# Spectral filter and mixer in one kernel: the first batch's row order, and where the length-64 sets and the u tile's parts stand

## The chip, the cores and the metric

The kernel runs on one core of a Trainium2 chip. The core's engines are TensorE (PE, matmuls; PEld is its weight load), VectorE (DVE), ScalarE (ACT), GpSimd (POOL) and SyncE (SP), which only issues DMAs here. Each engine works through its own instructions in the order in which the program gives them. The metric is the device time of one execution in microseconds (us).

## The reference, cut to what matters

x has 8 batches of 3008 rows (the sequence) by 256 columns. A real Fourier transform along the sequence is multiplied by a filter and transformed back; then comes one mixer layer over tokens and one over channels.

```python
X = np.fft.rfft(x, axis=1)                 # 8 x 1505 x 256
y = np.fft.irfft(X * (filt_r + 1j * filt_i)[None], n=3008, axis=1)
xt = y.transpose(0, 2, 1)
h = np.maximum(xt @ w_tok1, 0.0) @ w_tok2  # 3008 -> 256 -> 3008
u = y + h.transpose(0, 2, 1)
out = u + np.maximum(u @ w_ch1, 0.0) @ w_ch2   # 256 -> 1536 -> 256
```

x, the filter and the weights come in as float64 and are turned into float32 on the chip.

## The kernel before, in words

**Transform.** 3008 is 64 x 47. The transform is made in two stages, one of length 64 (tables `wa`, `was`) and one of length 47 folded to 24 (`wbi`), and goes back the same way; the last step, of length 64 again, is not made on its own but added into the u tile (`wai`). Batch 0 (`first`) runs alone at the start, while ScalarE, VectorE and TensorE also convert the weights to float32 (`convert_middle`, `convert_end`). Batch 1 uses whole 128-row matmuls (`a_unit`). Batches 2 to 7 are `tiled`: their length-64 stage consists of six *sets* (`a_pair`, called by `sets` in `dft`), each of eight matmuls on 64 x 64 quarters of the array, of which four run side by side. Ahead of each set VectorE makes a sum and a difference of the rows (`x_sums`, line 559, tile `sd`, two instructions; the sds lie alternately in two buffers). A set fills two PSUM banks, either those called acc and b (`turn`) or the two `pg` banks; ScalarE copies them out (line 550) and SP stores them to `z_tmp` (line 552).

**Rows of g.** What comes back from the length-47 stage is stored to `g_tmp` and read again as `t4` tiles of 128 rows. In before, all batches store these rows in two halves (`h k g`), the first batch too, which writes each piece with two DMAs from ScalarE's queue (line 697) and reads each part with two DMAs (`t4_load`, line 793).

**Mixer.** For each batch there are six tiles of output columns (m = 0 to 5, 512 wide, the last 448) and for each six steps over the hidden channels (jp = 0 to 5); an *item* is one (b, m, jp). In `mix`, an item issues on TensorE: `up_first` (line 1019, with u and v tiles into the pg banks), the first `down` part of the item before (line 1053, po banks, from hh), `up_last` (line 1035), and the second and third part of `down` (from t). VectorE (helper `v`, line 997) makes u2 (out: hh) and s from the pg banks, t from hh, and after `up_last` two additions "hh<-ps_pg,s", which free the pg banks; ScalarE applies the relu (line 1040).

**The u tile of the next m** is made meanwhile in parts by `u_quarter`: part 0 and 1 are pairs of matmuls (line 924), part 2 is `u_sets`, 32 small products on 64 x 64 quarters (line 904), and three pairs more; part 3 is empty. Then come `u_turn` (two VectorE steps on u) and `v_steps` (three on v), which wait in the list `todo_v` until `one_step` issues them. The v tile is what `up_first` of the next m needs after its first pair of matmuls. The tables `own` (same batch) and `new` (first m of the next batch) say at which place of which jp each part is issued. `finish` puts the steps that end an output tile into the same list.

**Token product.** Once a batch, at item n-4, `token_product` (line 850) goes through twelve blocks of token weights, which `w1_load` (line 827) brings from `w1_tmp` into a ring of seven.

**What sets the order.** The whole is under a manual schedule: every engine and every DMA queue keeps the order in which the Python code issues. `mix` yields at places 0, 1, 1.5, 1.7 and 2 of each item, and at each of these the table at the end (lines 1379 to 1381) decides whether the transform of a later batch, a generator, takes a step: "s" is one `x_sums`, "e" one set, "d" two sets, "c" the copies of the pair's acc and b banks. Before the change a tiled batch takes, in the last m of one batch, s at jp 3, 4, 5 and e at jp 4 and 5; in the first m of the next, s at jp 0, d at jp 1, c, s at jp 2 and 3, d at jp 4, c. `w_load` brings a filter tile, after `zero_rows` has cleared it on GpSimd (line 596).

**First batch's end.** `token_sums` (line 799) is its token product; `w2_load` (line 366) brings parts of w_tok2 through GpSimd's queue; `turn_out` (line 965) makes sums of w_tok2 on GpSimd.

Of the kernel before, what the change touches and what calls it, by code (L numbers as in the profile page):

```python
# [17 lines left out]
B = 8  # L18
# [41 lines left out]
def _make_tables():  # L60
# [12 lines left out]
    by_half = wai.reshape(K2, 2, 2, P).transpose(1, 0, 2, 3).reshape(P, P)  # L73
    wa, wait = wa.reshape(P, P), by_half.T
    wai = np.concatenate((by_half[:, one], by_half[:, two][:, ::-1]), axis=1)
# [46 lines left out]
    for e in range(2):  # L122
        for h in range(2):
# [4 lines left out]
            wbi.astype(f), wbi0.astype(f))  # L128
# [3 lines left out]
def kernel(  # L132
# [13 lines left out]
    wa_np, was_np, wa0_np, wai_np, wait_np, wbi_np, wbi0_np = _make_tables()  # L146
# [4 lines left out]
    wait_d = nc.inline_tensor(np.ascontiguousarray(wait_np), name="wait_t").ap()  # L151
    wbi_d = nc.inline_tensor(wbi_np, name="wbi_t").ap()
# [5 lines left out]
    z_d, g_d = ([nc.dram_tensor("%s_tmp%d" % (what, g), shape + (len(bs), D), FP32, kind="Internal").ap()  # L158
                 for g, bs in enumerate(GROUPS)] for what, shape in (("z", (P, A)), ("g", (2, K2, KH))))
# [367 lines left out]
    def rows_of(t_d, b):  # L527
        g, i = place_of[b]
        return t_d[g].rearrange("h k (g a) b d -> (h k g) a b d", a=A)[:, :, i, :]
# [42 lines left out]
    def dft(bs):  # L572
# [48 lines left out]
        def sets(i, n):  # L621
            return [a_pair(*u, sd, tags) for u, sd, tags in zip(todo[i:i + n], sums[i:], (turn, ("pg", "pg")))]

        if tiled:
            next_sum()
            yield "s"
            next_sum()
            for i in range(2):
                yield "e"
                sets(i, 1)[0]()  # L630
                yield "s"
                next_sum()
            for i in (2, 4):
                yield "d"
                leave, leave_pg = sets(i, 2)
                leave_pg()
                if i == 2:
                    zero_rows(0)
                    w_load(0)
                yield "c"  # L640
                leave()
                for _ in range(2 * (i == 2)):
                    yield "s"
                    next_sum()
            yield "w"
# [36 lines left out]
        def bi_unit(k):  # L682


            ps = bank(free_bank()).rearrange("p (b d) -> p b d", b=2)[:, 0:nb, :]
            for i, p in enumerate(prods.pop(k)):
                wi = turn_i[:, k // WC % 4, k % WC] if i else wbs[k // WC][:, TI:TI + 2 * KR:2, k % WC]
                nc.tensor.matmul(ps[0:KR], wi, p, start=(i == 0), stop=(i == 1))
            c, r = divmod(k, KC)
            if r == 0:  # L690
                where, tag = (p2p, "p2") if c % 3 == 2 else (t3p, "t3")
                t3s[c] = where.tile([KR, KC, nb, D], FP32, tag=tag, name="t3")
            by_block(t3s[c][:, r], ps[0:KR])
            if r == KC - 1:
                t3 = t3s.pop(c)
                for h in range(2):
                    nc.scalar.dma_start(g_d[0][h, ts(c, KC)].rearrange("k r b d -> r k b d"), t3[ts(h, KH)])
# [91 lines left out]
    def t4_load(b, c, lo=PARTS[0], hi=P, queue=nc.sync):  # L789
        if lo == 0:  # L790
            t4[b, c] = t4p.tile([P, TC4, D], FP32, tag="t4", name="t4")
        for to in [slice(lo, hi)] if hi - lo == P else [slice(h * HALF + lo // 2, h * HALF + hi // 2) for h in range(2)]:
            queue.dma_start(t4[b, c][to], rows_of(g_d, b)[to, ts(c, TC4), :])
# [32 lines left out]
    def w1_load(j):  # L826
        nc.sync.dma_start(w1_ring[:, j % W1S], w1_d[j])
# [129 lines left out]
    def w2_sums(m):  # L957
# [211 lines left out]
    def mix(next_ready):  # L1169
# [11 lines left out]
        own = ({(3, 0): (0,), (3, 2): (1,)}, {(2, 2): (0,), (3, 0): (1,), (3, 2): (2, 3)})  # L1181
        new = {(JP - 2, 0): (0, 1), (JP - 1, 0): (2, 3)}
# [20 lines left out]
        for i in range(len(items) + 1):  # L1203
# [84 lines left out]
    with tc.manual_schedule():  # L1288
# [71 lines left out]
        for b, i, place in mix(next_ready):  # L1360
# [57 lines left out]
```

## Time and profile before

| | us |
|---|---|
| three timed runs | 2429.73, 2432.22, 2433.08 (median 2432.22) |
| profiled execution | 2427.55 |
| its span, first to last instruction | 2425.7 |
| granted TensorE clock, mean | 0.993 |
| first mixer matmul at | 153 |
| one batch to the next (wait for v at 1032.2 and 1317.7) | 285.5 |

In the lines of the profile, L12 is line 12 of the kernel. A group reads: engine, line, operation, out<-in by tile names, partitions x elements, count. A timeline row begins with the start and the duration of the row in us; "x2" is two instructions merged into one row, and in brackets stands how long the engine had been idle before and what ended that. Float32 matmuls are recorded as two passes each. Matmuls overlap, so the step from one start to the next says what one costs: 0.216 us for a pass of 256 columns. Idle time of an engine that is not the bottleneck costs nothing.

### The profile page before, as it was taken

How to read it: one execution, taken by the hardware profiler on the slowest of the kernel's cores; microseconds unless marked ns; L12 is line 12 of the kernel's file. 1: busy time of each engine (PE TensorE's matmuls, PEld its weight loads, DVE VectorE, ACT ScalarE, POOL GpSimd, SP SyncE). 2: the span in 40 equal slices, each digit the busy share in tenths (PEclk: the TensorE clock that was granted, in tenths of full speed). 3: DMA queues.
4: the chain of work that ended last, by engine and by line, in shares of the span. 5: the costliest groups of instructions: out<-in, count | busy, mean ns of one | idle time of the engine just before them, and what ended most of it. 6: DMA issues, size and time to landing. Idle time of an engine off the chain costs nothing.

```text
span 2425.7 us, 41188 instructions
## 1 busy us (share of the span) xinstructions
PE 2366.4 (98%) x15148; PEld 1979.3 (82%) x15148; DVE 2006.1 (83%) x3753; ACT 689.4 (28%) x1339; POOL 708.8 (29%) x1138
## 2 busy tenths in 40 slices
PE   7899999999999999999999999999999999999998
PEld 4567788888897888978888888888889788898887
DVE  6788888788887888788887788878888798877887
ACT  5723222222223222232222222222222222212222
POOL 7465754131222122212212311321132113122122
PEclk8999999999999999999999999999999999999999
DMA  9774355533363334633435443634345433331101
GB/s 214 212 203 129 94 182 197 152 112 98 106 193 117 107 101 117 187 122 98 111 113 182 119 113 92 192 117 124 89 110 185 127 107 105 109 131 32 47 15 21
DMA packets 190143, 302.31 MB, mean 125 GB/s; under 512 B 43156, under 2 KB 126458, under 8 KB 184566
## 3 DMA queue, kind: packets, MB, share of 16 engines
q1 hardware_dynamic: 142942, 237.58, 31.9%
q0 software_dynamic: 40128, 55.28, 9.6%
q10 hardware_dynamic: 6872, 6.82, 0.9%
q8 instruction: 120, 1.97, 0.4%
q14 instruction: 81, 0.66, 0.1%
HBM read 215.37 MB, written 83.62 MB: 123 GB/s over the span
## 4 chain that ended last, share of the span: by engine, by line
PE 84%; DVE 3%; issue 0%; ACT 0%; DVEq 0%; ACTq 0%
PE ps_po L1053 33%; PE ps_pg L1019 19%; PE ps_pg L1035 14%; PE ps_acc L924 3%; PE ps_b L850 3%; PE ps_b L534 3%; PE ps_acc L850 2%; PE ps_pg L534 2%; PE ps_b L924 2%; PE ps_acc L904 2%; DVE u L997 1%; DVE hh L997 1%; DVE t L997 1%; DVE v L997 0%; PE ps_b L904 0%
## 5 line engine op out<-in xcount | busy, mean ns | idle before, releaser
L1065 POOL DMA_DIRECT2D out_dram<-r x738 | 453.2, 624 | 1386.1 <-issue 991.5
L1040 ACT ACTIVATE hh<-hh 128x512 f32<-128x512 f32 (+1 forms) x576 | 347.9, 621 | 1036.0 <-DVE hh L997 1032.1
L997 DVE TENSOR_TENSOR hh<-ps_pg,s 128x512 f32<-128x512 f32 (+3 forms) x864 | 481.9, 585 | 113.7 <-ACT s L1022 101.8
L1053 PE MATMUL ps_po<-t,wc 128*128 128x256 f32 (+1 forms) x2296 | 558.8, 380 | 0.9 <-DVE t L997 0.8
L1053 PEld LDWEIGHTS ps_po<-t,wc 128*128 128x128 f32 x2296 | 424.8, 190 | 99.2 <-issue 41.0
L1019 PE MATMUL ps_pg<-v,wc 128*128 128x256 f32 (+1 forms) x1728 | 419.0, 379 | 11.6 <-DVE v L997 11.6
L1053 PE MATMUL ps_po<-hh,wc 128*128 128x256 f32 (+1 forms) x1722 | 412.7, 376 | 0.6 <-POOL wc L393 0.6
L1019 PEld LDWEIGHTS ps_pg<-v,wc 128*128 128x128 f32 x1728 | 325.7, 191 | 61.6 <-DVE v L997 25.4
L1053 PEld LDWEIGHTS ps_po<-hh,wc 128*128 128x128 f32 x1722 | 328.0, 191 | 38.9 <-POOL wc L393 1.4
L1035 PE MATMUL ps_pg<-u,wc 128*128 128x256 f32 (+1 forms) x1152 | 292.3, 376 | 3.1 <-DVE hh L997 2.6
L997 DVE TENSOR_TENSOR t<-t,hh 128x256 f32<-128x256 f32 (+1 forms) x576 | 251.5, 437 | 19.8
L1035 PEld LDWEIGHTS ps_pg<-u,wc 128*128 128x128 f32 x1152 | 216.6, 190 | 36.5 <-DVE hh L997 10.3
L997 DVE TENSOR_TENSOR s<-ps_pg,hh 128x512 f32<-128x512 f32 (+1 forms) x288 | 196.1, 681 | 31.1 <-PE ps_pg L1019 0.8
L1022 ACT COPY s<-ps_pg 128x256 f32<-128x256 f32 (+1 forms) x288 | 106.0, 368 | 329.2 <-PE ps_pg L1019 327.7
L997 DVE TENSOR_TENSOR t<-hh 128x512 f32<-128x512 f32 (+1 forms) x288 | 195.1, 677 | 0.6 <-ACT hh L1040 0.6
L1019 PE MATMUL ps_pg<-u,wc 128*128 128x256 f32 (+1 forms) x576 | 169.7, 376 | 4.4 <-DVE hh L997 4.0
L1035 PE MATMUL ps_pg<-v,wc 128*128 128x256 f32 (+1 forms) x576 | 168.8, 375 | 0.0
L997 DVE TENSOR_TENSOR u<-ps_acc,u 128x256 f32<-128x256 f32 x84 | 46.8, 557 | 109.3 <-PE ps_acc L924 85.9
L1019 PEld LDWEIGHTS ps_pg<-u,wc 128*128 128x128 f32 x576 | 107.8, 190 | 22.0 <-DVE hh L997 8.5
L1035 PEld LDWEIGHTS ps_pg<-v,wc 128*128 128x128 f32 x576 | 108.7, 190 | 13.3 <-DVE s L997 0.4
L924 PE MATMUL ps_acc<-w 128*128 128x256 f32 x336 | 97.5, 392 | 0.0
L717 DVE TENSOR_TENSOR p<-ps_b,filt 128x1024 f32<-128x1024 f32 x56 | 68.4, 1222 | 14.2 <-PE ps_pg L534 13.3
(169 smaller groups left out, 2801.4 us busy)
## 6 DMA issues: line engine op xcount, KB each, us to landing
w<-w_tmp SPq DMA_DIRECT2D x42, 1024.0 KB
w<-w_tmp SPq DMA_DIRECT2D x84, 448.0 KB
out_dram<-r POOLq DMA_DIRECT2D x738, 32.0 KB, 4.0
g_tmp<-t SPq DMA_DIRECT2D x112, 192.0 KB
t<-g_tmp SPq DMA_DIRECT2D x42, 512.0 KB
t<-z_tmp SPq DMA_DIRECT2D x196, 96.0 KB
z_tmp<-t SPq DMA_DIRECT2D x72, 256.0 KB
wb<-wbi_t SPq DMA_DIRECT2D x56, 256.0 KB
```

Of the source, the lines that this page charges most:

```text
L534: nc.tensor.matmul(outs(i, j), stat(i, j), mov(i, j), start=True, stop=True)
L717: nc.vector.tensor_tensor(out=prods[c, h], in0=pss[h].unsqueeze(1).to_broadcast([P, 2, 2, D]), in1=filts[c % FB], op=ALU.mult)
L850: nc.tensor.matmul(ps[:, at], w[:, n], mov, start=(j == 0 and i in (0, 2)), stop=(j == AP - 1 and i >= 5))
L904: nc.tensor.matmul(pss[e][half_of(i), dh, ts(q, HALF)], t4[b, c][half_of(e), r, ds(dh * P + i * HALF, HALF)], wai[half_of(e), 0:HALF], sta ...
L924: nc.tensor.matmul(to, h1[:, n, :], w2_at(m, at), start=(i < 2 and j == 0), stop=(j >= 1))
L997: nc.vector.tensor_tensor(out=out, in0=in0, in1=in1, op=op)
L1019: nc.tensor.matmul(ps[:, 0:hw], chan[0][:, jp, n, :], mov, start=True, stop=True)
L1022: nc.scalar.copy(out=s[:, 0], in_=g[0][:, 0, 0:hw])
L1035: nc.tensor.matmul(ps[:, 0:hw], chan[0][:, jp, n, :], mov, start=True, stop=True)
L1040: nc.scalar.activation(out=hs, in_=hs, func=AF.Relu)
L1053: nc.tensor.matmul(po[i][:, j, 0:hw], chan[1][:, jp, n, :], mov, start=(jp == 0 and first == 1), stop=(jp == JP - 1 and last == 1))
L1065: q.dma_start(bass.AP(tensor=ob.tensor, offset=ob.offset + to, ap=ap + [[1, cw]]), of)
```

## The change

It has these parts:

1. The first batch keeps the order `(k, g)` of its rows; the table `wai` (and its transpose, with which w_tok1's conversion multiplies) follows. Writing and reading `g_tmp` takes one DMA instead of two. At item 28 the first 64 columns of `wai` are overwritten with the table for the later batches (`was_i`).
2. Later batches still use two halves, so `w1_load` reads the token weights with rows permuted, in two DMAs of 64 partitions.
3. `turn_out` does in three instructions what took six.
4. Parts 2 and 3 of the u tile (the 32 small products) are issued at place 1.5, between the second and the third part of `down`: for the same batch at jp 3 instead of jp 3 place 2, for the next batch at jp 4 instead of jp 5 place 0. Two `one_step` calls follow at jp 4 of the last m.
5. The six sets are taken as one, two, one, two instead of one, one, two, two. The two single ones stand at the places of part 4, right ahead of the small products, in the pg banks instead of acc and b. The sums are taken at jp 3 of the last m and at jp 0, 1, 2, 3, 4 of the first m. The clearing and loading of the first filter tile follows the fourth sum.

```diff
         if tiled:
             next_sum()
-            yield "s"
-            next_sum()
-            for i in range(2):
+            for i in (0, 3):
                 yield "e"
-                sets(i, 1)[0]()
-                yield "s"
-                next_sum()
-            for i in (2, 4):
+                sets(i, 1, (("pg", "pg"),))[0]()
+                for _ in range(2 if i == 0 else 1):
+                    yield "s"
+                    next_sum()
                 yield "d"
-                leave, leave_pg = sets(i, 2)
+                leave, leave_pg = sets(i + 1, 2, (turn, ("pg", "pg")))
                 leave_pg()
-                if i == 2:
-                    zero_rows(0)
-                    w_load(0)
                 yield "c"
                 leave()
-                for _ in range(2 * (i == 2)):
+                for _ in range(2 * (i == 0)):
                     yield "s"
                     next_sum()
+                    if len(sums) == 4:
+                        zero_rows(0)
+                        w_load(0)
...
-                t3 = t3s.pop(c)
-                for h in range(2):
-                    nc.scalar.dma_start(g_d[0][h, ts(c, KC)].rearrange("k r b d -> r k b d"), t3[ts(h, KH)])
+                nc.scalar.dma_start(g_d[0][ts(c, KC)].rearrange("k r b d -> r k b d"), t3s.pop(c))
...
-        for to in [slice(lo, hi)] if hi - lo == P else [slice(h * HALF + lo // 2, h * HALF + hi // 2) for h in range(2)]:
-            queue.dma_start(t4[b, c][to], rows_of(g_d, b)[to, ts(c, TC4), :])
+        queue.dma_start(t4[b, c][lo:hi], rows_of(g_d, b)[lo:hi, ts(c, TC4), :])
...
     def w1_load(j):
-        nc.sync.dma_start(w1_ring[:, j % W1S], w1_d[j])
+        rows = w1_d[j].rearrange("(k h g) s n -> h k g (s n)", h=2, g=2)
+        for h in range(2):
+            nc.sync.dma_start(w1_ring[half_of(h), j % W1S], rows[h])
...
         def turn_out():
-            for t in range(2):
-                pool(halves_of[:, t, 1], halves_of[:, t, 0], halves_of[:, t, 1])
-                pool(halves_of[:, t, 0], halves_of[:, t, 0], halves_of[:, t, 0], ALU.add)
-                pool(halves_of[:, t, 0], halves_of[:, t, 0], halves_of[:, t, 1])
+            pool(two, one, two)
+            pool(one, one, one, ALU.add)
+            pool(one, one, two)
...
-        own = ({(3, 0): (0,), (3, 2): (1,)}, {(2, 2): (0,), (3, 0): (1,), (3, 2): (2, 3)})
-        new = {(JP - 2, 0): (0, 1), (JP - 1, 0): (2, 3)}
+        own = ({(3, 0): (0,), (3, 2): (1,)}, {(2, 2): (0,), (3, 0): (1,), (3, 1.5): (2, 3)})
+        new = {(JP - 2, 0): (0, 1), (JP - 2, 1.5): (2, 3)}
...
             yield b, i % n, 1.5
+            if now:
+                u_parts(b, m, jp, 1.5)
             if old:
                 down(mo, jo, 2, hhs.pop(i - 1), tts.pop(i - 1), pos[bo, mo])
...
                 u_parts(b, m, jp, 2)
+                if m + 1 == MT and jp == JP - 2 and b + 1 < B:
+                    one_step()
+                    one_step()
...
+                if i == 28:
+                    nc.sync.dma_start(wai[:, 0:HALF], was_i_d)
...
-                    "s": ((3, 1), (4, 1), (5, 1)) if tail else ((0, 1), (2, 1), (3, 1)),
-                    "e": ((4, 1.5), (5, 1.5)), "d": ((1, 1.5), (4, 1.5)), "c": ((2, 0), (5, 0)),
+                    "s": ((3, 1),) if tail else ((0, 1), (1, 1), (2, 1), (3, 1), (4, 1)),
+                    "e": ((4, 1.5),) if tail else ((3, 1.5),), "d": ((1, 1.5), (4, 1.5)), "c": ((2, 0), (5, 0)),
```

More of the change, by code (lines that the diff above doesn't have):

```diff
@@ L72, in _make_tables @@
         wai[k2] = wa[:, k2].T * (2.0 if k2 else 1.0)
-    by_half = wai.reshape(K2, 2, 2, P).transpose(1, 0, 2, 3).reshape(P, P)
-    wa, wait = wa.reshape(P, P), by_half.T
-    wai = np.concatenate((by_half[:, one], by_half[:, two][:, ::-1]), axis=1)
+    wait = wai.reshape(P, P).T
+    was_i = wai.reshape(K2, 2, 2, P).transpose(1, 0, 2, 3).reshape(P, P)[:, one]
+    wa, wai = wa.reshape(P, P), wai.reshape(P, P)
+    wai = np.concatenate((wai[:, one], wai[:, two][:, ::-1]), axis=1)
     n1 = A - 1 - np.arange(A)
@@ L127, in _make_tables @@
     return (wa.astype(f), np.concatenate((wa[one], wa[one])).astype(f), wa0.astype(f), wai.astype(f), wait.astype(f),
-            wbi.astype(f), wbi0.astype(f))
+            was_i.astype(f), wbi.astype(f), wbi0.astype(f))
 @with_exitstack
@@ L144 @@
     nc = tc.nc
-    wa_np, was_np, wa0_np, wai_np, wait_np, wbi_np, wbi0_np = _make_tables()
+    wa_np, was_np, wa0_np, wai_np, wait_np, was_i_np, wbi_np, wbi0_np = _make_tables()
     wa_d = nc.inline_tensor(wa_np, name="wa_t").ap()
@@ L151 @@
     wait_d = nc.inline_tensor(np.ascontiguousarray(wait_np), name="wait_t").ap()
+    was_i_d = nc.inline_tensor(np.ascontiguousarray(was_i_np), name="was_i_t").ap()
     wbi_d = nc.inline_tensor(wbi_np, name="wbi_t").ap()
@@ L157 @@
     place_of = {b: (g, i) for g, bs in enumerate(GROUPS) for i, b in enumerate(bs)}
-    z_d, g_d = ([nc.dram_tensor("%s_tmp%d" % (what, g), shape + (len(bs), D), FP32, kind="Internal").ap()
-                 for g, bs in enumerate(GROUPS)] for what, shape in (("z", (P, A)), ("g", (2, K2, KH))))
+    z_d, g_d = ([nc.dram_tensor("%s_tmp%d" % (what, g), shape[g > 0] + (len(bs), D), FP32, kind="Internal").ap()
+                 for g, bs in enumerate(GROUPS)]
+                for what, shape in (("z", ((P, A), (P, A))), ("g", ((K2, KR), (2, K2, KH)))))
     w2_d = nc.dram_tensor("w2_tmp", (MT, P, 4, 512), FP32, kind="Internal").ap()
@@ L528, in rows_of @@
         g, i = place_of[b]
-        return t_d[g].rearrange("h k (g a) b d -> (h k g) a b d", a=A)[:, :, i, :]
+        rows = "h k (g a) b d -> (h k g) a b d" if g else "k (g a) b d -> (k g) a b d"
+        return t_d[g].rearrange(rows, a=A)[:, :, i, :]
     def four(outs, stat, mov):
@@ L619, in next_sum, with sets @@
             more(1)
-        def sets(i, n):
-            return [a_pair(*u, sd, tags) for u, sd, tags in zip(todo[i:i + n], sums[i:], (turn, ("pg", "pg")))]
+        def sets(i, n, banks_of):
+            return [a_pair(*u, sd, tags) for u, sd, tags in zip(todo[i:i + n], sums[i:], banks_of)]
         if tiled:
             next_sum()
-            yield "s"
-            next_sum()
-            for i in range(2):
+            for i in (0, 3):
                 yield "e"
-                sets(i, 1)[0]()
-                yield "s"
-                next_sum()
-            for i in (2, 4):
+                sets(i, 1, (("pg", "pg"),))[0]()
+                for _ in range(2 if i == 0 else 1):
+                    yield "s"
+                    next_sum()
                 yield "d"
-                leave, leave_pg = sets(i, 2)
+                leave, leave_pg = sets(i + 1, 2, (turn, ("pg", "pg")))
                 leave_pg()
-                if i == 2:
-                    zero_rows(0)
-                    w_load(0)
                 yield "c"
                 leave()
-                for _ in range(2 * (i == 2)):
+                for _ in range(2 * (i == 0)):
                     yield "s"
                     next_sum()
+                    if len(sums) == 4:
+                        zero_rows(0)
+                        w_load(0)
             yield "w"
```

## The prediction

> **What bounds the kernel now.** I read the page first: busy shares, then the chain of work that ended last.
>
> ```profile
> PE 2366.4 (98%) x15148; PEld 1979.3 (82%) x15148; DVE 2006.1 (83%) x3753; ACT 689.4 (28%) x1339; POOL 708.8 (29%) x1138
> PE 84%; DVE 3%; issue 0%; ACT 0%; DVEq 0%; ACTq 0%
> ```
>
> TensorE is the bound, so a gain must come from its idle gaps, its array switches, or the first 150 us, which have other limits. The order of the built program shows the same 7576 matmuls and 3755 VectorE instructions after the change: work is moved, not removed. So I looked for what TensorE waits on (its own waits, longest of each kind last):
>
> ```profile
> PE ps_pg L1019 <- DVE v L997: 11.6, 7, 1.7
> ```
>
> Seven waits for v: one at each change of batch. The timeline there, TensorE then VectorE, for batch 2 to 3:
>
> ```profile
> 1032.20 0.59 PE L1019 MATMUL ps_pg<-u,wc 128*128 128x256 f32 x2
> 1034.53 1.56 PE L1019 MATMUL ps_pg<-v,wc 128*128 128x256 f32 x6 [1.74 <-DVE v L997]
> ...
> 1029.74 1.15 DVE L997 TENSOR_TENSOR hh<-ps_pg,s 128x448 f32<-128x448 f32 x2
> 1032.12 1.28 DVE L559 TENSOR_TENSOR sd<-filt 128x512 f32<-128x512 f32 x2
> 1033.33 0.68 DVE L997 TENSOR_TENSOR v<-u 128x512 f32<-128x512 f32 x1
> ```
>
> Without the wait the v matmuls would follow the u pair after 0.43 us; they come 2.33 after it: 1.90 lost. Between hh and v stand two u steps and a pair of sums (sd). Six of the seven look like this; the last (batch 6 to 7, no sets beside it) is different:
>
> ```profile
> 2172.95 0.67 PE L1019 MATMUL ps_pg<-u,wc 128*128 128x256 f32 x2 [0.48 <-DVE u L997]
> 2174.76 2.47 PE L1019 MATMUL ps_pg<-v,wc 128*128 128x256 f32 x6 [1.15 <-DVE v L997]
> ...
> 2175.28:2178.69 3.41, 3.41 (x10) 0.50 0.01 2
> ```
>
> After two gaps the granted clock is 0.50 for 3.41 us (last line, a stretch of the windows view: busy, clock, DMA share, GB/s). By start-to-start times TensorE loses there 0.65 and 1.39 waiting, then 0.97 and 0.82 at half clock: 3.8.
>
> **The change, part by part.** All steps below are start-to-start times of that timeline.
>
> *1. Batch change, six times.* u's parts 2 and 3 and the two u_turn steps come an item earlier, and two sums leave this stretch. From 1020.37, where the first down matmuls of item jp=4 start (0.85 with the switch to 64-row tiles, to 1021.22): the set now uses the pg banks, which the hh pair (1020.57 + 1.15 = 1021.72) must leave first, so its second half starts at 1021.78. Set 0.86 + 0.05, u's 32 small products 1.09, its three full pairs 1.40, down 0.76: 1025.94. Item jp=5 has 5.29 (1.51 + 1.135 + 1.135 + 1.51), then the u pair 0.43: TensorE is ready for v at 1031.66. VectorE: u adds and u_turn from 1025.36 for 1.21 + 1.32, to 1027.89; that is 0.58 later than hh could start (1.37 after 1025.94), so hh, s and the t sums end at 1030.31 (+2.42), hh pair 1.06, first v 0.72, second 0.44 + 0.06: v is there at 1032.59. TensorE still waits 0.93, but goes on at 1032.59 instead of 1034.53: -1.94. One set less is done by then; it returns in step 3.
>
> *2. First pair of sets in the new batch (jp=1).* Before, sums and sets are an item apart. Now the second set's sum is issued at (1, 1) and the pair at (1, 1.5), and VectorE's built order puts it behind hh and three finish steps:
>
> ```profile
> 1045.25 1.28 DVE L997 TENSOR_TENSOR hh<-ps_pg,s 128x512 f32<-128x512 f32 x2
> 1046.45 1.22 DVE L997 TENSOR_TENSOR u<-u,r 128x224 f32<-128x224 f32 x3
> ...
> 1046.50 1.16 PE L534 MATMUL ps_pg<-sd,was 64*64 64x512 f32 x8
> ```
>
> Both engines keep their distance from the v matmuls, so before's clock serves. The sum can start at 1046.45 + 1.13 = 1047.58 and ends, at 1.28 for two, at 1048.86. TensorE wants the second set at 1046.50 and all but its first quarter waits until 1048.92, then 0.86 + 0.16: down goes on at 1049.94 instead of 1047.59: +2.35. Queued behind on TensorE are the down matmuls and the whole next item.
>
> *3. The single set beside u's small products (3, 1.5).* New on this path: 0.86 + 0.05. It shares the switches of the small products (about 0.09 in and 0.22 out when a set stands alone). Its pg banks are free when the hh pair ends:
>
> ```profile
> 1060.70 1.28 DVE L997 TENSOR_TENSOR hh<-ps_pg,s 128x512 f32<-128x512 f32 x2
> ```
>
> 1062.04 against TensorE's 1061.61: 0.43. Together +1.34.
>
> *4. Second pair (jp=4).* The same as step 2; here hh and the two u_turn steps stand ahead of the sum:
>
> ```profile
> 1071.05 0.69 DVE L950 SCALAR_TENSOR_TENSOR u<-u 128x512 f32<-128x512 f32 x1
> ...
> 1071.14 1.04 PE L534 MATMUL ps_pg<-sd,was 64*64 64x512 f32 x8
> ```
>
> The sum runs 1071.65 to 1072.93, the set from 1072.99, down at 1074.01 instead of 1072.11: +1.90.
>
> Per batch -1.94 + 2.35 + 1.34 + 1.90 = +3.65; six batches: +21.9. Bounds: if VectorE were in time at both pairs, steps 2 and 4 are 0 (-3.6 in all); if each pair of sums takes the 1.54 that the one at 1014.90 took instead of 1.28, +25.0. I take the chain, whose durations are from the same items.
>
> *5. Batch 6 to 7.* No sums or sets. The chain of step 1 leaves a wait of 0.92 for 3.8 now lost (the clock window included): -2.9; ends 0 and -3.8.
>
> *6. First batch.* ScalarE has no gap between 35 and 112 us when its DMA issues are counted:
>
> ```profile
> 92.57 0.36 ACT L700 COPY t<-ps_acc 96x256 f32<-96x256 f32 x1
> 92.96 0.83 ACTq L697 DMA_DIRECT2D g_tmp<-t  x2
> 93.84 0.59 ACT L333 COPY w<-ps_po 128x512 f32<-128x512 f32 x1 [0.90 <-PE ps_pg L674]
> ```
>
> One of each pair of issues goes: about 0.42 x 16 = 6.9 at most. TensorE's round there (4.88 start to start) holds 4.16 of streaming, and 0.3 to 0.4 of the rest is its wait for VectorE's second product, so I take 0.33 a round: 5. Then GpSimd:
>
> ```profile
> 113.92 3.24 POOL L793 DMA_DIRECT2D t<-g_tmp  x6 [8.55 <-DMA g_tmp<-t]
> 117.15 2.16 POOL L366 DMA_DIRECT2D st<-in_moe_w_tok_dram  x4
> ```
>
> Three issues fewer, 1.6 us, ahead of weight loads that ScalarE then waits 7.36 for; SP issues 21 loads instead of 42, three fewer after the last write at about 0.7 each (26 in 18.67), so TensorE's token sums start 2.1 earlier. Since VectorE's conversions follow the weights, I take 1.6. Together -6.6; ends 0 (DMA is at 0.85 there and may be what comes next) and -9.1.
>
> *7. Costed at nothing.* Token weights in two halves: 84 more SP issues of 0.45; five pairs a batch precede the x loads, 2.3 us, and the first sum (1014.90) needs only loads issued by 1002.5; without that cover 2.3 a batch. GpSimd's w2 sums (36 fewer, 18 larger) are waited for by no TensorE row. The filter tile's memset and its eleven SP loads come an item later, before two z stores: used at 1090.6, issued by about 1073; the stores land 2 us later, just ahead of ScalarE's next copies into those buffers (1072 + 2.3); if late, up to 1 a batch. One 64-column load: 0.4 of SP.
>
> Sum: 21.9 - 2.9 - 6.6 = +12.4. The profiled execution took 2427.55 (span 2425.7), so 2440.0 on its scale; it is 4.7 below the median 2432.22, and on that scale the forecast is 2444.
>
> *Two rules of the Trainium skill.* The row: the clock halved after gaps of 0.48 and 1.15 inside one 3.41 us window, and it didn't after six single gaps of 1.74. "TensorE: Matmul & The Clock Gate", section "HAM oscillation — how this bites in real kernels", warns of idle gaps above about 3.4 us only. By it the new waits never cost clock, and the sum stands; by the row each could cost a window more, 1.8. Against the change speaks "DMA: Bandwidth & Descriptors", "Rules for kernel authors": a transfer in two partition halves gains nothing, one of 128 partitions is better. By it the token weights' split is pure cost; the rows show it covered, and by an estimate from the page's fixed 2 us a DMA, with no cover, it would add 2 for each of 84.
>
> **Rivals.**
> - *Faster.* VectorE reaches the sums before TensorE reaches the pairs. It decides at 1046.5: the sum must end 2.4 us earlier than my chain has it. For it: VectorE has idle gaps of 1 to 3 us in neighbouring items. Against: hh, which stands ahead of the sum, itself ends after the pair has begun (1046.53 against 1045.59). Then -0.60 x 6 - 2.9 - 6.6 = -13: 2419.
> - *No change.* The sums run half as late: 1.2 and 0.95 gone from steps 2 and 4, -12.8 in all: 2432.
> - *First batch gives nothing,* because the DMA engines (0.85 busy) feed no faster: +19: 2451.
> - *The clock drops* in the waits of step 2 (1.7 of idle each, from the first set's end at 1046.6 to the first of the two sums; the window that dropped held 0.65 + 1.39): 6 x 1.8 = +10.8: 2455.
> - That the change doesn't do what it says is excluded by the built order: set and small products are adjacent.
>
> **Numbers.** My chain 0.50, first batch nothing 0.18, clock 0.12 (all slower), no change 0.11, faster 0.09. Its own range is 2440 to 2451: steps 5 and 6 at their best give +9, slow sums and half of step 6 give +19. To leave out no more than 2 in 10, the range runs from just below the no-change case to just above the clock case, 2430 to 2458. 0.2% of 2432, 4.9 us, is about what can be told from no change: slower 0.80, same 0.11, faster 0.09.
>
> **What would show it.** TensorE waits in L534 for sd (L559), 12 times, around 2.3 and 1.8 us; waits for v at the batch change near 0.9, seven times; no half-clock window near 2175; the first mixer matmul some 6 us earlier than 153. Wrong if TensorE's L534 rows show no wait for sd, or if the first stage keeps its length.

## The result, and the profile after

The changed kernel takes 2457.0 us (median of four, 2449.61 to 2460.43) against 2430.97 for the kernel before on the same chip: a ratio of 1.0104, 95% interval 1.0078 to 1.013. It is slower by 26 us. The profiled execution took 2460.43 (span 2458.7), 32.9 more than the one before; it lies at the top of its four, so the items below add up to more than the medians differ by.

The busy shares and the chain, from the page of the changed kernel, answer to the first two lines shown of before:

```profile
PE 2379.9 (97%) x15148; PEld 1983.3 (81%) x15148; DVE 2011.5 (82%) x3753; ACT 689.4 (28%) x1339; POOL 705.6 (29%) x1117
PE 71%; DVE 10%; DMA 9%; POOL 4%; issue 3%; ACT 2%; SPq 1%; DVEq 0%; ACTq 0%; POOLq 0%
```

TensorE is still the bound, but the chain leaves it more often: DVE from 3% to 10%, DMA from nothing to 9%. What it waits for now (engine, line, released by: us in all, times, longest):

```profile
PE ps_pg L538 <- DVE sd L563: 17.4, 12, 1.7
...
PE ps_pg L1035 <- DVE hh L997: 7.3, 10, 1.6
PE ps_pg L1019 <- DVE v L997: 5.3, 7, 0.8
...
PE ps_pg L1019 <- ACT t L554: 2.8, 6, 1.1
PE ps_b L851 <- DMA w<-w_tmp: 2.4, 4, 0.9
```

The seven waits for v have fallen from 11.6 to 5.3, and twelve waits for sd, a wait that did not exist, cost 17.4. At the change from batch 2 to 3, TensorE and then VectorE:

```profile
1041.06 0.60 PE L1019 MATMUL ps_pg<-u,wc 128*128 128x256 f32 x2
1042.41 0.92 PE L1019 MATMUL ps_pg<-v,wc 128*128 128x256 f32 x3 [0.76 <-DVE v L997]
...
1040.16 1.15 DVE L997 TENSOR_TENSOR hh<-ps_pg,s 128x448 f32<-128x448 f32 x2
1041.22 0.68 DVE L997 TENSOR_TENSOR v<-u 128x512 f32<-128x512 f32 x1
```

v now follows hh directly; the two u steps and the pair of sums that stood between are gone. A pair of sums stands in the second item of the new batch instead (batch 2):

```profile
763.62 0.59 PE L538 MATMUL ps_acc<-sd,was 64*64 64x512 f32 x2
765.95 1.59 PE L538 MATMUL ps_pg<-sd,was 64*64 64x512 f32 x8 [1.73 <-DVE sd L563]
...
763.99 1.22 DVE L997 TENSOR_TENSOR u<-u,r 128x224 f32<-128x224 f32 x3
765.12 1.28 DVE L563 TENSOR_TENSOR sd<-filt 128x512 f32<-128x512 f32 x2
```

The first set is done and the second waits for a sum that VectorE begins only after the three finish steps.

To say where the rest went, I take the start of the first u matmul (line 1019, or the same statement in the experiments) of each of the 288 items in both traces and compare the length of each item. Items not in the table agree within 0.4 us.

| part (profiled executions, after minus before) | us | predicted |
|---|---|---|
| start of the mixer (153.1 to 140.7) | -12.4 | -6.6 |
| batch 0's mixer, without its token product | +8.0 | 0 |
| token product and the item behind it, batch 0 / batches 1 to 5 | +2.6 / +6.5 | 0 / 0 |
| batch change, six times -1.89 | -11.3 | -11.6 |
| batch change 6 to 7 | -2.7 | -2.9 |
| first pair of sets (and the item behind it), six times | +18.7 | +14.1 |
| single set beside u's products, six times 1.28 | +7.7 | +8.0 |
| second pair (and the item behind it), six times | +15.8 | +11.4 |
| sum | +32.9 | +12.4 |

In the first pair 14.0 are six times 2.33. The other 4.7 are three windows of half clock right behind the wait, in batches 1, 3 and 4. From the windows view (stretch; us and busy of PE, PEld, DVE, ACT and POOL; then clock, DMA share, GB/s):

```profile
474.30:477.71 3.41, 3.41 (x11) 1.51 (x5) 0.00 (x0) 1.07 (x2) 0.00 (x0) 0.50 0.41 111
...
1058.00:1061.41 3.41, 3.41 (x9) 2.66 (x10) 0.00 (x0) 0.99 (x2) 0.00 (x0) 0.50 0.58 183
1351.50:1354.91 3.41, 3.41 (x12) 1.80 (x6) 0.00 (x0) 1.07 (x2) 0.00 (x0) 0.50 0.41 118
```

### The profile page after: what moved, and what is told of

It reads as the page before. It is cut to its first block, busy times and chain, and to the rows that moved or that the text cites. A ratio compares the mean times of both kernels' runs of the same rounds, so it can differ in the third digit from the quotient of the medians.

```text
span 2458.7 us, 41273 instructions
## 1 busy us (share of the span) xinstructions
PE 2379.9 (97%) x15148; PEld 1983.3 (81%) x15148; DVE 2011.5 (82%) x3753; ACT 689.4 (28%) x1339; POOL 705.6 (29%) x1117
## 3 DMA queue, kind: packets, MB, share of 16 engines
q8 instruction: 120, 1.97, 0.4%
## 4 chain that ended last, share of the span: by engine, by line
PE 71%; DVE 10%; DMA 9%; POOL 4%; issue 3%; ACT 2%; SPq 1%; DVEq 0%; ACTq 0%; POOLq 0%
PE ps_po L1053 28%; PE ps_pg L1019 16%; PE ps_pg L1035 12%; PE ps_acc L925 3%; DVE t L997 3%; PE ps_pg L538 3%; PE ps_b L538 2%; POOL out_dram L1065 2%; DMA z_tmp<-t 2%; DVE hh L997 2%; PE ps_b L925 2%; DMA out_dram<-r 1%; DVE u L997 1%; PE ps_b L851 1%; PE ps_acc L905 1%
## 5 line engine op out<-in xcount | busy, mean ns | idle before, releaser
L1053 PE MATMUL ps_po<-t,wc 128*128 128x256 f32 (+1 forms) x2296 | 566.8, 381 | 3.4 <-DVE t L997 3.3
L997 DVE TENSOR_TENSOR s<-ps_pg,hh 128x512 f32<-128x512 f32 (+1 forms) x288 | 196.0, 681 | 30.7 <-DVE hh L997 0.9
L717 DVE TENSOR_TENSOR p<-ps_b,filt 128x1024 f32<-128x1024 f32 x56 | 68.4, 1222 | 14.5 <-PE ps_pg L538 11.4
```

What stands on the lines that cost most here:

```text
L717: nc.vector.tensor_tensor(out=prods[c, h], in0=pss[h].unsqueeze(1).to_broadcast([P, 2, 2, D]), in1=filts[c % FB], op=ALU.mult)
L997: nc.vector.tensor_tensor(out=out, in0=in0, in1=in1, op=op)
L1053: nc.tensor.matmul(po[i][:, j, 0:hw], chan[1][:, jp, n, :], mov, start=(jp == 0 and first == 1), stop=(jp == JP - 1 and last == 1))
```

## The experiments

My theory was the prediction's chain: VectorE's late sums are the loss, the batch change and the first batch the gain, loads are hidden. The rivals that the trace after suggests: the rows' side (two-part weight loads, long GpSimd sums) carries a loss of its own; and the waits for sd only stand in front of others that would take their place.

### Rows alone, schedule alone

`rows_only` keeps parts 1 to 3 of the change and takes the sums, sets and places of before; `sched_only` is the opposite.

> Only the row order of the first batch, the two-part weight loads, the three long GpSimd sums and the added 64-column load; sums, sets and u's parts as before. My prediction's steps 6 and 7 say: 6.6 us earlier from the first batch, nothing elsewhere, so about 2424 where before has 2431. The reading of the two traces says otherwise: mixing starts some 12 us earlier, about 10.6 us of that is lost again inside batch 0, the token product pays 2.7 us more in batch 0 and about 1.1 in each of the five batches after it: a sum of -12.4 + 10.6 + 2.7 + 6.5 = +7, near 2438. If it comes out below 2428, the losses in batch 0 belong to the schedule and not to the rows.

> Only the schedule: the two sets of length 64, the sums' and u parts' new places, the early steps at the batch change; rows, weights and GpSimd as before. By the items of the trace after: six times -1.89 and once -2.7 at the batch change, six times 2.33 for the wait for the sum and three times 1 to 1.6 for half-clock windows in it, six times 1.28 for the single set beside u's products, six times about 2.3 for the second pair: -14.0 + 14.0 + 3.7 + 7.7 + 14 = +25, near 2456. By the prediction's own prices (1.90 for the second pair, no windows, batch change -14.5) it is +19, near 2450. If it were below 2445, the schedule's waits would need the later token weights or GpSimd's longer sums to be as long as they are.

Measured: rows alone 2429.1 (ratio 1.0002, 0.9993 to 1.0011), schedule alone 2453.9 (1.0108, 1.0094 to 1.0121). The schedule is the whole loss, +25 as the items had it; it shows the same -1.89, 2.35 (once 2.00), 1.28 and 2.1 or more with the old loads. It has the same six waits of 1.7 at the first pairs and no half-clock window behind any of them, so the windows of the changed kernel are not a fixed part of its price. The rows come out even, neither my 2424 nor the 2438. Their items say why: mixing starts 12.3 earlier, 7.5 of that is lost in batch 0's mixer, 3.8 in its token product and 6.3 at the next five (product and the item behind it). All of these losses are there with the old schedule, so they belong to the rows.

### Token weights in two transfers

```diff
-        nc.sync.dma_start(w1_ring[:, j % W1S], w1_d[j])
+        for h in range(2):
+            nc.sync.dma_start(w1_ring[half_of(h), j % W1S], w1_d[j, half_of(h)])
```

> The kernel before with each 448 KB load of the later batches' token weights cut into two transfers of 64 partitions, nothing else. My step 7 costs that at nothing (2431, bound 2.3 a batch if uncovered, 16 in all). The trace after shows waits for these weights of 2.4 us in 4 waits, and the token product longer by 0.7 to 2.1 us in each batch: by that it is +6 to +9, near 2438. If it is within 2 us of before, the longer token product comes from other transfers that meet the weights' (the sets' new places), not from the cut.

Measured: 2439.8 (1.0048, 1.0035 to 1.0061), 11 us for nothing but the cut. Batch 0's token product is 6.2 longer; at the next five, product and the item behind it are 4.7 longer together; the last, in batch 6, where no x loads follow, keeps its length. The windows view over batch 1's product and the item behind it, of before and then of this run:

```profile
701.50:728.50 27.00, 27.00 (x213) 26.98 (x212) 19.81 (x55) 2.44 (x6) 10.49 (x18) 1.00 0.86 268
```

```profile
710.50:738.00 27.50, 27.27 (x211) 26.49 (x210) 19.39 (x54) 2.35 (x7) 9.86 (x16) 1.00 0.94 263
```

There was little room to begin with: the DMA engines are 0.86 busy there before. With the loads halved they are 0.94 busy and move no more, 263 GB/s for 268. TensorE, without a gap before, now has some.

Only in batch 0 does TensorE wait for the weights themselves (3.7 in four waits). In batches 1 to 5 the product keeps its 24.15 us, and the loss stands in the item behind it. ScalarE and TensorE of this run there, batch 2:

```profile
1021.30 0.27 ACT L859 COPY c<-ps_b 128x128 f32<-128x128 f32 x1 [20.24 <-DMA out_dram<-r]
...
1023.23 1.02 PE L1036 MATMUL ps_pg<-u,wc 128*128 128x224 f32 x4 [0.77 <-DVE hh L998]
```

ScalarE copies the product's result into a buffer that a store of output rows must free first. In before it starts this copy as the product ends; here it starts 1.65 us later. The last sixteen of these stores take 6.5 us from issue to landing on average, where they took 5.0. VectorE goes on with the copy, its hh is late by as much, and TensorE waits for hh. The changed kernel has the same wait: hh at line 1035, 2.6 before and 7.3 after. Whether the stores land later because of the busier DMA engines alone was not tested apart.

`rows_single` is the other direction: the row change with the weights stored in the later batches' order already, so that each load is one transfer again. `parts` has four entries, each 32 rows of `w1_d` and every fourth partition of `w`.

```diff
-            nc.gpsimd.dma_start(to[:, :, 0], w[:, :, 0, 0])
-            nc.gpsimd.dma_start(to[:, :, 1:3], w[:, :, 1])
+            for to, of in parts:
+                nc.gpsimd.dma_start(to[:, :, 0], w[of, :, 0, 0])
+                nc.gpsimd.dma_start(to[:, :, 1:3], w[of, :, 1])
...
-        rows = w1_d[j].rearrange("(k h g) s n -> h k g (s n)", h=2, g=2)
-        for h in range(2):
-            nc.sync.dma_start(w1_ring[half_of(h), j % W1S], rows[h])
+        nc.sync.dma_start(w1_ring[:, j % W1S], w1_d[j])
```

> The row change alone, with the token weights written to DRAM already in the later batches' row order (each store becomes four of 32 partitions on GpSimd's queue, in batch 0 only), so that each later load is one transfer of 128 partitions again. By the runs: the halves cost 3.8 us in batch 0's token product and 0.6 to 1.9 in those of batches 1 to 5 here (6.4 together), so -10 if the loads are the cause and the 72 more GpSimd issues (some 0.6 us each, beside batch 0) are hidden: near 2419. If GpSimd's issues hold up w2's sums in batch 0, part of it is given back there; if the product is slow because other transfers meet the weights', it stays at 2429.

Measured: 2421.4 (0.9971, 0.9959 to 0.9982). All token products and the items behind them are back to the length of before within 0.04 us. The additional stores (24, not the 72 of the expectation) cost nothing that shows: batch 0's mixer loses 6.8 here and 7.5 in `rows_only`.

### GpSimd's three long sums

`turn_three` joins them in the kernel before, `rows_six` splits them again in the row change.

```diff
-            for t in range(2):
-                pool(halves_of[:, t, 1], halves_of[:, t, 0], halves_of[:, t, 1])
-                pool(halves_of[:, t, 0], halves_of[:, t, 0], halves_of[:, t, 0], ALU.add)
-                pool(halves_of[:, t, 0], halves_of[:, t, 0], halves_of[:, t, 1])
+            pool(two, one, two)
+            pool(one, one, one, ALU.add)
+            pool(one, one, two)
```

> The kernel before with only those six GpSimd instructions joined to three, nothing moved otherwise. Theory A: the same items 8, 12, 16 and 17, 20, 24, 28 lengthen and batch 0 ends some 5 us later, near 2434. Theory B: nothing, 2428 to 2430.

> The row change alone (the run before this: 2429.1 where before had 2428.8), with GpSimd's first sums of each group of w2 again in six instructions of 128x256 instead of three of 128x512. There batch 0 gave back 7.4 us of the 12.3 that mixing starts earlier in its mixer, 5.7 of them in the items where these sums run (12: 1.62, 17: 1.43 with 16: 0.23, 28: 2.19, 8: 0.21). Theory A (a GpSimd instruction of twice the length holds VectorE up): those 5.7 come back, near 2423. Theory B (the losses come from mixing earlier, against the same pace of loads and conversions): no change, 2428 to 2430.

Measured: `turn_three` 2435.5 (1.0026, 1.0015 to 1.0037). Its batch 0 grows by 6.1, in the items of the changed kernel and by its amounts (12: 1.61, 17: 1.43, 28: 2.19). In `rows_six` these amounts are gone (-1.62, -1.43, -2.14). Its median, 2427.6 (0.9995, 0.9986 to 1.0004), can't be told from that of `rows_only` and by itself stands with theory B: the two-part loads, still there, vary by more from run to run. A median without them is that of `rows_bound` below, which has the short sums. Batch 0's mixer loses 3.4 in `rows_six`, against 7.5 in `rows_only`; 1.8 of these 3.4 stand in its first item, and their cause was not pursued. Before, item 12, VectorE:

```profile
258.50 0.98 DVE L722 TENSOR_TENSOR p<-p,p 128x512 f32<-128x512 f32 x1
...
262.65 1.97 DVE L997 TENSOR_TENSOR t<-t,hh 128x256 f32<-128x256 f32 x2
264.54 1.27 DVE L997 TENSOR_TENSOR hh<-ps_pg,s 128x512 f32<-128x512 f32 x2
```

The same in `turn_three`: GpSimd, VectorE, TensorE:

```profile
261.92 4.61 POOL L965 TENSOR_TENSOR w<-w 128x512 f32<-128x512 f32 x3
...
259.08 2.02 DVE L722 TENSOR_TENSOR p<-p,p 128x512 f32<-128x512 f32 x1
...
264.26 2.55 DVE L996 TENSOR_TENSOR t<-t,hh 128x256 f32<-128x256 f32 x2
266.74 1.28 DVE L996 TENSOR_TENSOR hh<-ps_pg,s 128x512 f32<-128x512 f32 x2
...
262.89 1.13 PE L1034 MATMUL ps_pg<-u,wc 128*128 128x256 f32 x4 [0.98 <-DVE hh L996]
266.87 0.70 PE L1052 MATMUL ps_po<-t,wc 128*128 128x256 f32 x2 [0.70 <-DVE t L996]
```

VectorE's operations from SBUF to SBUF that are shown (p, t) take 2.02 and 2.55 where they took 0.98 and 1.97, and TensorE waits for them; that from PSUM (hh) keeps its 1.27. GpSimd gains little by it: until batch 0 ends its sums at line 965 take 44.2 us, where they took 47.4 before. How the loss divides between the length of these sums and where they fall is open: the 2.02 lies beside GpSimd's sums of 128x384, the 2.55 beside the long ones. What the two runs show, item by item, is that the joining alone makes and unmakes the loss. In the Trainium skill, "SBUF — State Buffer", section "SBUF: two separate sides", speaks of an exclusive lock: a VectorE operation with two SBUF inputs and a GpSimd operation that reads SBUF share a port pair, and whoever comes second is blocked for the other's whole instruction. The single records of batch 0's mixer agree. Of the additions "t<-t,hh" of batch 0, those that start while one of GpSimd's sums or differences runs, 22 in before and 19 in `turn_three`, all end 0.28 or 0.29 us after that sum; those that start beside one of its memsets or DMA issues keep their 0.43, but for one in each run. By that a longer sum holds an addition that meets it for longer.

### Stores of the first batch

```diff
-                nc.scalar.dma_start(g_d[0][ts(c, KC)].rearrange("k r b d -> r k b d"), t3s.pop(c))
+                t3 = t3s.pop(c)
+                for h in range(2):
+                    nc.scalar.dma_start(g_d[0][ts(c, KC), ts(h, KH)].rearrange("k r b d -> r k b d"), t3[ts(h, KH)])
```

> The run rows_six (2427.6; mixing starts 12.5 us earlier than before) with each store of the first batch's tiles on ScalarE's queue cut into two again, rows as in the change. My step 6 prices the store alone: 5.0 of ScalarE's time. By that mixing starts 5 us later than in rows_six, at -7.5 against before, and the time is near 2432. Rival (the rest of 12.5 is the load of the same tiles and the DMA engines, which move 254 GB/s there instead of 238): if the loads in one piece make the gain, the start stays within 2 us of -12.5; if the stores make all of it, it goes back to about 0.

Measured: mixing starts at -8.2 against before, 4.3 later than in `rows_six`; 2432.5 (1.0019, 1.001 to 1.0028). The store is worth 4.3 by the starts and 4.9 by the medians, near my 5.0. These starts are of one execution each, and kernels with the same first stage differ there by 2 to 3 us (-12.3 to -14.3 with the new rows, 0 to +2.9 with the old). The rest, 8.2, lies on the reading side. GpSimd's queue in this run:

```profile
114.02 1.53 POOL L796 DMA_DIRECT2D t<-g_tmp  x3 [8.64 <-DMA t<-g_tmp]
...
124.30 1.50 POOL L404 DMA_DIRECT2D st<-in_moe_w_ch_dram  x3 [3.54 <-issue]
```

and in the changed kernel, with one store:

```profile
110.01 1.55 POOL L792 DMA_DIRECT2D t<-g_tmp  x3 [9.16 <-DMA g_tmp<-t]
...
120.29 1.50 POOL L404 DMA_DIRECT2D st<-in_moe_w_ch_dram  x3 [5.01 <-issue]
```

and before, where the last rows' loads began at 113.92:

```profile
131.05 3.99 POOL L401 DMA_DIRECT2D st<-in_moe_w_ch_dram  x8 [10.19 <-issue]
```

From the last rows to the first channel weights it is 10.3 us in both runs with loads in one piece and 17.1 before, 6.8 less, and to the start of the mixer 30.7 and 30.8 against 39.2, 8.4 less. My step 6 put 1.6 on the reading side. Why fewer loads bring that much more was not taken apart.

### The waits for sd, and what stands behind them

`sums_early` issues the sums earlier in the changed kernel:

```diff
-                    "s": ((3, 1),) if tail else ((0, 1), (1, 1), (2, 1), (3, 1), (4, 1)),
+                    "s": ((3, 1), (5, 1)) if tail else ((0, 1), (2, 1), (3, 1), (4, 0)),
```

> The changed kernel with the sums before the filter's sets issued earlier on VectorE: the second sum in the last item but one half of the batch before, the third at the first item, the sixth one place earlier; sets and u's parts stay. Theory (TensorE's wait for the sum sd is the cost of both pairs): the six waits of 2.33 and their half-clock windows (3.7 together) go, and about 1.5 of the 2.3 of each second pair: 14 + 3.7 + 9 = 27 us less than the changed kernel, near 2430. Rival (VectorE is behind by that much anyway, and the wait only moves to hh and v): less than 10 us, above 2447.

Measured: 2443.7 (1.006, 1.0046 to 1.0074), between the two. The first pair falls from 2.33 to 0.32 with its windows, as the theory says. The second pair does not move: 2.07 and more, with no wait for sd left. GpSimd, SP, ScalarE and TensorE around it, batch 2:

```profile
768.43 8.54 POOL L1065 DMA_DIRECT2D out_dram<-r  x14 [37.38 <-issue]
776.95 1.86 POOL L600 MEMSET filt<- 128x1024 f32 x2
...
777.95 0.34 SPq L233 DMA_DIRECT2D filt<-in_filt_r_dram  x1
...
781.85 1.14 SPq L556 DMA_DIRECT2D z_tmp<-t  x2
...
775.50 1.07 ACT L554 COPY t<-ps_pg 128x512 f32<-128x512 f32 x2
...
788.84 0.58 ACT L554 COPY t<-ps_pg 128x512 f32<-128x512 f32 x1 [2.54 <-DMA z_tmp<-t]
...
789.48 0.81 PE L1019 MATMUL ps_pg<-u,wc 128*128 128x256 f32 x2 [1.65 <-ACT t L554]
```

ScalarE has copied the single set out by 776.57. SP can't store the two copies before 781.85: the filter's loads stand ahead of them in its queue and wait for GpSimd's memset, which starts only when GpSimd has issued fourteen output stores in a row. So the next copies find both t1 tiles taken, the pg banks stay full, and `up_first` waits 1.65. Two of the six waits have a half-clock window behind them. Against `sums_early`, `filter_behind` changes this order and nothing else:

```diff
                 sets(i, 1, (("pg", "pg"),))[0]()
+                if i:
+                    zero_rows(0)
+                    w_load(0)
...
                     next_sum()
-                    if len(sums) == 4:
-                        zero_rows(0)
-                        w_load(0)
```

> The changed kernel with the early sums of the run sums_early, and with the zeroing of the first filter tile and its twelve loads put behind the single set's stores in SP's queue, where they stood ahead of them. In sums_early the wait for the sum was gone from the second pair, but the pair still cost 2.07 to 2.95 us: ScalarE's copies wait for the t1 tiles, whose stores SP issues at 781.85, 5 us after the single set's copies, behind filter loads that start only after GpSimd's memset. Theory (the place in SP's queue is the second pair's price): the fifth items fall from about +2.3 to +0.5 or less against before, six times 1.7 and two half-clock windows of 1.7, some 10 to 14 us less than sums_early: near 2431. Rival (the bank copies on ScalarE are late for another reason, or the filter loads are now late for the first filter product): within 3 us of sums_early's 2443.7.

Measured: 2430.5 (1.0007, 0.9998 to 1.0015), the 2431 of the theory. The second pair costs 0.57 in all six batches, without a window. The memset starts at the same place of the batch as in `sums_early` (31.4 after its start). In its trace the stores go first and the next copies do not wait:

```profile
771.75 0.81 SPq L556 DMA_DIRECT2D z_tmp<-t  x2
...
773.58 0.44 SPq L233 DMA_DIRECT2D filt<-in_filt_r_dram  x1
...
781.90 1.17 ACT L554 COPY t<-ps_pg 128x512 f32<-128x512 f32 x2
```

So the second pair of the changed kernel had two things late side by side, the sum and the stores, and with the sum in time the stores alone kept its price up. The loads put behind with the sums as late as they were was not tried.

### The batch change alone, and what beats both kernels

`boundary_only` puts u's last part and the two early steps into the kernel before:

```diff
-        new = {(JP - 2, 0): (0, 1), (JP - 1, 0): (2, 3)}
+        new = {(JP - 2, 0): (0, 1), (JP - 2, 1.5): (2, 3)}
...
+            if now:
+                u_parts(b, m, jp, 1.5)
...
+                if m + 1 == MT and jp == JP - 2 and b + 1 < B:
+                    one_step()
+                    one_step()
```

> The kernel before with only the next batch's last u part moved to the fifth item's second half and the two early VectorE steps behind it; sums, sets, rows and loads as before. By the batch changes of the changed kernel's trace (2.76 - 3.68 - 0.97 six times, -2.67 at the last one): -11.3 - 2.7 = -14.0, near 2415. My prediction's step 1 and 5 say -14.5. Against it: with the old places of the sets, one single set stands where u's part now goes and a second one an item later; each meeting like the one in the middle of the batch costs 1.28, so if the second set meets the moved steps too, six times that, near 2423.

Measured: 2422.5 (0.9976, 0.9965 to 0.9986), -6.2: not the 2415 of the theory, but the 2423 of the objection. Here six of the seven waits for v are gone, but the single set before u's products fills the banks that these take next, and TensorE waits 1.16 for ScalarE's copies: each change gives 0.70, not 1.89. This and the rows with single transfers and six short sums make `rows_bound`:

> The two parts that each proved faster, together: the first batch's row order with single transfers for the token weights and six short GpSimd sums, and the early end of u's parts at the batch change; sums and sets of before. If they add: rows_single gave -7.3, six short sums take another 5.3 from batch 0, the batch change gave -6.2: 2428.7 - 18.8, near 2410. If the starts' gain is lost to the same waits that end batch 0 anyway, it stays at 2415 or above.

Measured: 2410.0 (0.9928, 0.9916 to 0.9939). The parts add, and this version is faster than both kernels. What `rows_single` and `boundary_only` gave, 7.3 and 6.2, leaves some 5 of its gain for the short sums, as against the 6.1 that `turn_three` lost by the long ones. The last run moves u's part behind the third part of `down`, so that ScalarE has time for its copies:

```diff
-        new = {(JP - 2, 0): (0, 1), (JP - 2, 1.5): (2, 3)}
+        new = {(JP - 2, 0): (0, 1), (JP - 2, 2): (2, 3)}
```

> The run rows_bound (2410.0) with u's last part at the batch change one group of products later, behind the third group of the fifth item instead of ahead of it. In rows_bound TensorE waits 1.16 us there, six times, for ScalarE's copies of the two banks that the single set has just written and u's products take next. Theory: the four products between (0.86) cover most of that wait, about 0.3 stays and two more changes between products of 64 and of 128 rows cost 0.2: some 0.7 less in each of six batch changes, near 2406. Rival: u's sums end later by as much, and the wait for v at the next batch's first item, gone in rows_bound, comes back: 2410 or above.

Measured: 2412.0 (0.9925, 0.9911 to 0.9939), no difference. TensorE's waits in `rows_bound`:

```profile
PE ps_acc L910 <- ACT t L554: 7.0, 6, 1.2
...
PE ps_pg L1041 <- DVE hh L1003: 3.1, 6, 1.1
```

and in `rows_bound_late`:

```profile
PE ps_pg L1041 <- DVE hh L1003: 7.7, 14, 1.1
...
PE ps_acc L910 <- ACT t L554: 1.2, 6, 0.2
```

The wait for the banks is gone and one for hh has come in the next item: -0.76 in one, +0.75 in the other, six times. Neither of my two accounts had it: not v but hh was late, one step of VectorE earlier.

## Why the prediction was right, and where it was wrong

The forecast, 2444 with 0.80 for slower, had the sign and its main mechanism; the measured 2457.0 lies at the upper end of its range. That it lies inside is in part luck: the upper end was set by the clock rival, of whose 10.8 only 4.7 came, and the rest is the balance of a gain and of losses that the sum had too small or not at all. Step by step:

1. *Batch change, six times -1.94:* measured -1.89, the wait for v as foretold. Its mechanism holds.
2. *First pair, +2.35:* measured 2.33, and `sums_early` shows that the sum is the cause. What failed is that I kept the clock out of the sum: the rival gave each of the six waits a window, three had one (and none in `sched_only`), and they cost 1.3 to 1.7 where I took 1.8.
3. *Single set beside u's products, +1.34:* measured 1.28, with and without the new loads. Its split into waits was not tested.
4. *Second pair, +1.90:* measured 2.23 to 3.18, and 0.10 in the item behind it. The step named one late thing, the sum; the stores were late as well.
5. *Batch 6 to 7, -2.9:* measured -2.7, no half clock there any more. Some 1.7 of it is that window, which before's profiled execution had by chance: of the seven kernels with the old order at this change, four show no window there.
6. *First batch, -6.6, ends 0 and -9.1:* mixing starts 12.4 earlier, outside my ends. The store term was right (5.0, measured 4.3); the reading term was too small (1.6, measured 8.2, of which 6.8 up to the channel weights). I had counted the issues saved on GpSimd and on SP; what the weights behind them gain beyond that was in no term.
7. *Costed at nothing:* wrong in three of four. The token weights' two halves were given the cover of the x loads behind them, on SP's issues. The first sum was in time, as the step says; what came late were the weights themselves, above all in batch 0, and in the next five the output stores that free ScalarE's buffer, on DMA engines already 0.86 busy: 9.1 in the changed kernel. GpSimd's sums "are waited for by no TensorE row", which is true and beside the point: they slow VectorE, which TensorE waits for; 6.1 in `turn_three`. The rows of before already showed it, the pair of t sums at 1.97 beside GpSimd's sums and at 0.88 elsewhere. The filter loads ahead of two stores, "if late, up to 1 a batch": 1.5 a batch once the sums are early (2.07 to 0.57). The 64-column load shows nowhere.

Step 6 was short by 5.8 of gain and step 7 by about 17 of loss; with steps 2 and 4 short by 9, that makes the profiled executions' 33 out of 12.

On the two rules weighed there: "DMA: Bandwidth & Descriptors", "Rules for kernel authors", against transfers in two partition halves, is borne out, with 11 us for 84 cut loads, a fraction of the 2 us each of the prediction's estimate. (The page gives its fixed cost in the section "Anatomy of one DMA — SWDGE (gpsimd) path", for DMAs issued from GpSimd; these are issued from SP.) The warning in "TensorE: Matmul & The Clock Gate", "HAM oscillation — how this bites in real kernels", of gaps above some 3.4 us does not cover this case: gaps of 1.73 to 1.74 halved the clock three times.

The rivals: *faster* and *no change* would need the sums in time, and the trace has them late. *First batch gives nothing* came true in its effect, not by its reason: the mixer did start earlier, and gave the gain back to GpSimd's sums and to the token weights.

## What to carry to other kernels

Before a transfer is cut or moved at no charge, look at the DMA share of the stretch where it is used, and list what is behind it in the queue and beside it on the DMA engines, and whose buffers that frees: here a cut load was paid for by a copy that waited for an output store. Where a step has two late releasers, removing one shows little until the other is found, so follow the next one before the first fix is called useless. An engine that nobody waits for can still cost, by slowing one that somebody waits for.

## What the runs showed of the hardware

- The half clock comes on a grid. The three windows above begin 583.70 and 293.50 apart, 171.0 and 86.0 times 3.413, the length of such a window in the clock records. By the clock records of the fourteen profiled executions, every window after the first stage lies on such a grid, and none follows a stretch of the grid that TensorE's rows fill by more than 0.53. Of 36 stretches filled by less (0.37 to 0.52), 11 were followed by half clock, 25 not. So a gap of 1.74 may cost 1.7 more or nothing: the six equal waits for v at the batch changes never halved the clock in before and twice in `turn_three`, while the last change, with its two gaps, did so in before and not in `turn_three`. In `sched_only` only one of the six waits at the first pairs falls into a single stretch of the grid, and none was followed by half clock. What decides among the 36 is open.
- VectorE's operations from SBUF to SBUF can lengthen beside GpSimd's sums: the pair "t<-t,hh" of 128x256 takes 0.88 in batch 2, where GpSimd sums nothing, and 1.97 to 2.55 beside its sums in batch 0. Those that read PSUM keep their time ("hh<-ps_pg,s", 1.27 and 1.28). Those additions that meet a GpSimd sum end 0.28 or 0.29 after it (22 of 22 in before, 19 of 19 in `turn_three`), as by the lock named above.
- A DMA issue on ScalarE's queue holds ScalarE itself: two in a row 0.80, one 0.31, and the first batch's round followed it, from 4.84 to 4.37.
